# A merged weight conversion, fewer summing transfers and other times for side work, in a kernel of attention and two expert networks

## The chip, the core and the metric

The kernel runs on one core of a Trainium2 chip. A core has TensorE (matmuls, into PSUM), VectorE and ScalarE (elementwise work), GpSimd and a queue of transfers on SyncE. The metric is the device time of one execution, in microseconds (us). Times are compared as medians of repeated runs on the same chip.

## What is computed

Attention over 4 batches of 8 heads, 576 tokens and 64 columns each, in which every score below the row's maximum less tau is dropped, and behind it two networks on all 2304 tokens. The weights come as 64-bit floats.

```python
scores = scale * np.matmul(q, k.transpose(0, 1, 3, 2))
thresh = np.max(scores, axis=-1, keepdims=True) - tau
scores = np.where(scores >= thresh, scores, -1000000000.0)
...                                    # softmax, then
x = np.matmul(attn, v)                 # (2304, 512)
h = x @ w_in                           # (512, 2048)
x = (np.maximum(h, 0) + alpha * np.minimum(h, 0)) @ w_out
h = x @ w2_in
out = (h * (1 / (1 + np.exp(-h)))) @ w2_out
```

## The kernel before, in words

**Attention.** 16 pairs of heads, each with 9 tiles of 128 rows, so 144 steps. A step takes its scores on TensorE (L596), scales them and finds the maximum on VectorE (L610, 576 elements from PSUM), takes the exponential on ScalarE (L623) and masks and sums on VectorE (L636). Transposes (L670) and the products with v (L704, L711) follow. TensorE's order is the table ORDER; the function plan places the other engines' work by costs and priorities.

**Networks.** Tokens are in three blocks of 768 (p), the hidden layer in four groups of 512 (g), so each network (m) has 12 blocks of work, 24 in all. Both matrix products of a block are done by a scheme of seven products in place of eight: L482 runs 12 matmuls of 384 columns for each of the seven, on operands that are sums and differences of quarters. The first group of the first network alone has its second product done plainly (L966). Every 32-bit operand is split in two parts of reduced precision: a copy on ScalarE (L322) and the difference (the "split", L433 for weights, L472 for x, L1018 for the hidden layer), which may run on VectorE or GpSimd (both_step); three products of parts are summed.

**Weights.** Each group has eight chunks (four of w_in, four of w_out), 64 in all. The function conv turns a chunk's 64-bit floats into 32 bits: the magnitude's upper word through Abs with a scale on ScalarE (L404, into its own tile cm), the low word's top bits (L405), the sign put in (L407) and the joining of both (L409), then four sums of 128 columns (L428, one of them L422 in some chunks) and two splits of 384 and 512 columns (L433). A plain chunk has one split of 512 (L415). Seven chunks are converted during the attention, beside its own work; WI, WS, WN and WT say at which steps. XO says from which step on the first pieces of x may be made there (L463 the differences, L472 their splits); plan chooses the engine.

**Order in the networks.** TensorE's order is fixed by the loops. The function plan_late orders the rest by due times: a step is due when its TensorE user is, less what follows it, less OFF of its kind. It gives a both_step to GpSimd only with enough slack (POOL_SLACK), or, where PK allows, when much else waits for VectorE. Instructions marked port=True and GpSimd's work are kept apart by it, as users of one port. In the first network some sums of hidden tiles (acc, L1024) are not made by an engine but by a transfer that accumulates (L1029, issued from GpSimd); DSUM names which. Pieces of x are stored to DRAM in group 0 (L1117) and loaded again in the later groups (L1119), through four or five buffers xs.

## Time and profile before

| | us |
|---|---|
| median of 3 runs | 1019.19 (1013.49 to 1019.28) |
| profiled execution | 1022.07 |
| its span, first to last instruction | 1020.3 |
| TensorE busy in the span | 995.0 |
| VectorE busy | 899.1 |
| ScalarE busy | 658.9 |
| GpSimd busy | 214.5 |
| mean granted TensorE clock | 0.991 of full |

Matmuls are pipelined and their ends are modelled, so a busy TensorE is not one at its peak; counting matmuls in a stretch shows more. In the rows below PE is TensorE, PEld its weight loads, DVE VectorE, ACT ScalarE and POOL GpSimd; a row's `out<-in` names tiles, and L numbers are lines of the kernel. An arrow `<-` in a list of waits leads to the engine and line that ended the wait.

### The profile page before, as it was taken

Reading aid. Unit: us, or ns where it says so; the run is one execution under the profiler, and the core shown is the slowest. Engines: PE = TensorE matmul, PEld = TensorE weight load, DVE = VectorE, ACT = ScalarE, POOL = GpSimd, SP = SyncE. Lnnn points to the kernel's source line nnn. Section 1 sums busy time; section 2 is a strip of 40 time slices with the busy share of each in tenths; the row PEclk is TensorE's granted clock in tenths of the full one; section 3 lists DMA queues with packets and bytes.
Section 4 is the critical chain, followed back from the end, with each engine's and each line's share of the span. In section 5 each row is a group of like instructions: output and inputs, shape, how many; then the busy total and the mean of one; then the engine's idle time right before and its main releaser. Section 6 shows DMA issues by size and latency. Waiting matters only on the chain.

```text
span 1020.3 us, 16812 instructions
## 1 busy us (share of the span) xinstructions
PE 995.0 (98%) x6045; PEld 881.8 (86%) x6045; DVE 899.1 (88%) x1928; ACT 658.9 (65%) x1252; POOL 214.5 (21%) x163
## 2 busy tenths in 40 slices
PE   9999999999999998999999999889999999999998
PEld 5666665666579998999999999889999999999997
DVE  7999999999789876989799989799998999989666
ACT  6898888888776755555465546577676556555442
POOL 0000100000013102442533443522212231222011
PEclk9999999999999999999999999899999999999999
DMA  3222222221565776687777776455677776664743
GB/s 113 75 100 90 85 69 85 87 67 45 200 239 212 262 282 197 212 288 273 258 250 262 230 270 220 168 220 196 230 275 248 249 256 224 230 237 170 250 164 109
DMA packets 46916, 196.41 MB, mean 193 GB/s; under 512 B 5488, under 2 KB 8688, under 8 KB 46832
## 3 DMA queue, kind: packets, MB, share of 16 engines
q1 hardware_dynamic: 43936, 187.97, 51.7%
q0 software_dynamic: 2592, 7.08, 3.8%
q8 instruction: 48, 0.79, 0.3%
q10 hardware_dynamic: 304, 0.28, 0.1%
q14 instruction: 36, 0.29, 0.1%
HBM read 150.48 MB, written 37.75 MB: 184 GB/s over the span
## 4 chain that ended last, share of the span: by engine, by line
PE 84%; DVE 9%; DMA 3%; ACT 2%; issue 2%; ACTq 0%; DVEq 0%
PE ab L482 25%; PE c L482 16%; PE y L482 15%; PE s L596 8%; PE t L670 7%; PE pv L704 6%; PE y L966 5%; DMA xs<-xd 2%; DVE e L636 1%; DMA r<-r 1%; PE t L711 1%; DVE x L610 1%; PE t L676 1%; DVE xs L472 1%; DVE g L1018 1%
## 5 line engine op out<-in xcount | busy, mean ns | idle before, releaser
L482 PE MATMUL ab<-xs,w 128*128 128x384 f32 x1728 | 316.7, 337 | 7.7 <-DMA xs<-xd 3.9
L482 PEld LDWEIGHTS ab<-xs,w 128*128 128x128 f32 x1728 | 301.6, 189 | 12.6 <-issue 3.9
L482 PE MATMUL y<-g,w 128*128 128x384 f32 x840 | 159.6, 338 | 0.9 <-DVE X L983 0.9
L482 PEld LDWEIGHTS y<-g,w 128*128 128x128 f32 x840 | 149.5, 191 | 1.2 <-DVE X L983 1.2
L322 ACT ACTIVATE g<-r 128x768 fp32r<-128x768 f32 (+1 forms) x143 | 111.9, 795 | 50.3 <-PE c L482 15.9
L1018 POOL TENSOR_TENSOR g<-r,g 128x768 fp32r<-128x768 f32 x47 | 86.7, 1848 | 189.6 <-DVE ce L407 60.4
L482 PE MATMUL c<-g,w 128*128 128x384 f32 x612 | 117.0, 339 | 4.3 <-DVE g L1018 4.3
L610 DVE TENSOR_SCALAR_CACHE_REDUCE x<-s,nsc 128x576 f32<-128x576 f32 x144 | 112.6, 816 | 7.1 <-PE s L596 6.7
L322 ACT ACTIVATE su<-ab 128x384 f32<-128x384 f32 x144 | 70.1, 489 | 74.6 <-PE ab L482 69.8
L482 PEld LDWEIGHTS c<-g,w 128*128 128x128 f32 x612 | 108.1, 190 | 5.4 <-DVE g L1018 5.2
L983 DVE TENSOR_TENSOR X<-y,X 128x384 f32<-128x384 f32 x150 | 81.2, 552 | 27.8 <-PE y L482 27.6
L623 ACT ACTIVATE e<-x,m 128x576 f32<-128x576 f32 x128 | 96.7, 785 | 8.5 <-DVE x L610 8.3
L596 PE MATMUL s<-raw 64*128 64x288 f32 (+1 forms) x576 | 101.0, 429 | 0.6 <-DVE x L610 0.5
L636 DVE SCALAR_TENSOR_TENSOR e<-x,m,e 128x577 f32<-128x577 f32 x128 | 100.2, 813 | 1.1 <-ACT m L630 1.1
L596 PEld LDWEIGHTS s<-raw 64*128 64x128 f32 (+1 forms) x576 | 57.7, 188 | 38.9 <-DVE x L610 11.0
L482 PE MATMUL c<-xs,w 128*128 128x384 f32 x432 | 83.2, 341 | 3.5 <-ACT r L937 3.0
L322 ACT ACTIVATE pt<-t 128x512 f32<-128x512 f32 x128 | 70.5, 605 | 17.7 <-PE t L670 17.4
L482 PEld LDWEIGHTS c<-xs,w 128*128 128x128 f32 x432 | 77.1, 192 | 4.4 <-ACT r L937 3.3
L670 PEld LDWEIGHTS t<-ident,e 128*128 128x128 f32 x576 | 63.2, 141 | 20.2 <-issue 8.9
L670 PE MATMUL t<-ident,e 128*128 128x128 f32 x576 | 79.4, 278 | 0.2 <-DVE e L636 0.2
L1018 DVE TENSOR_TENSOR g<-r,g 128x768 fp32r<-128x768 f32 x74 | 71.3, 966 | 8.2 <-ACT g L322 7.9
L704 PE MATMUL pv<-pt,rv 128*64 128x512 f32 x256 | 62.4, 604 | 0.0
(110 smaller groups left out, 1447.6 us busy)
## 6 DMA issues: line engine op xcount, KB each, us to landing
xs<-xd SPq DMA_DIRECT2D x126, 768.0 KB, 6.1
xd<-xs SPq DMA_DIRECT2D x42, 768.0 KB, 3.6
raw<-in_w1i SPq DMA_DIRECT2D x16, 512.0 KB, 5.2
raw<-in_w1o SPq DMA_DIRECT2D x16, 512.0 KB, 4.7
raw<-in_w2i SPq DMA_DIRECT2D x16, 512.0 KB, 4.4
raw<-in_w2o SPq DMA_DIRECT2D x16, 512.0 KB, 4.3
rv<-in_v SPq DMA_DIRECT2D x16, 480.0 KB, 3.6
r<-r POOLq DMA_DIRECT2D x18, 384.0 KB, 7.5
```

Source lines behind the costliest of these rows:

```text
L322: e.activation(out=dst, in_=src, func=AF.Copy)
L472: st.append(both_step(2 * HN, src[1] + key, key, lambda e: e.tensor_tensor(out=xtile(slot)[:, 1], in0=src[0](), in1=xtile(slot)[:, 0].bitc ...
L482: T.matmul(bank, WT_[ws[c]][:, x, AI[a], :], xs[:, y, c, :], start=start and k == 0, stop=stop and k == 5, skip_group_check=True,)
L596: T.matmul(SP[u + k][:, hf, :S // 2], RAW[i][p, 0, q], RAW[i][p, 1, c], start=True, stop=True)
L610: V.tensor_scalar(out=x.rearrange("p (a b) -> p a b", a=2), in0=SP[u][:, :, :S // 2], scalar1=nsc, scalar2=None, op0=ALU.mult, op1=ALU.min ...
L623: A.activation(out=ES[u], in_=xts[u % XB][:, 1:S + 1], func=AF.Exp, bias=mcol(u, 0), scale=-1.0)
L636: V.scalar_tensor_tensor(out=e, in0=x, scalar=mcol(u, 1), in1=e, op0=ALU.is_le, op1=ALU.mult, accum_out=mcol(u, 2))
L670: T.transpose(TP[n][:, c * 128:(c + 1) * 128], EP[i, t // 2][:, o:o + 128], ident)
L704: T.matmul(AV[i][h * 64:(h + 1) * 64], RV[i][:, h, kt], src, start=kt == 0, stop=kt == KT - 1)
L966: T.matmul(yt, wview(ws[f])[:, a, i * 128:(i + 1) * 128], half(gs[f, k])[:, c], start=n == 0, stop=n == 3 * G - 1)
L983: V.tensor_tensor(out=dst, in0=src, in1=dst, op=ALU.add))))
L1018: add(*both_step(2 * HN, kr + kg, kg, lambda e: e.tensor_tensor(out=x[:, 1], in0=RP[n], in1=x[:, 0].bitcast(F32), op=ALU.subtract)))
```

## The change

The four parts of a chunk and its four sums now lie in one tile cw of eight columns of 128, of which cv and ce are the two halves. Abs writes into cv itself. L407, a two-source operation on 32-bit words, becomes a one-source operation on 16-bit halves (L408 of after), and L405 (L406) works on 16-bit halves too: one fills the lower half of each word, the other the upper. Two of the four sums, which subtract the same part, become one of 256 columns, except in the chunks with L422. One copy and one split of 896 columns, over seven neighbouring columns of cw, replace two each. So that these lie side by side, the host's order of the parts, the order of the seven weight operands (AI) and the signs of two differences of x are changed; weights are tracked by one key in place of two.

DSUM now goes by group: accumulating transfers make 12 of the sums where they made 18. The attention's seven chunks start at steps 34 to 94, ten apart, and the first pieces of x may start at step 114 instead of 84. The planner's due times and its rules for GpSimd have new numbers. TensorE's order is the same but for six matmuls of a first-network product that stand some 90 matmuls earlier in the attention's last steps.

```diff
@@ -33,13 +33,13 @@
-WI = 20
-WT = 4
+WI = 34
+WT = 12
...
-WS = 14
-WN = 6
-XO = 60
+WS = 10
+WN = 7
+XO = 30
...
-DSUM = (7, 4)
+DSUM = ((), (4,), (4,), (6, 4))
...
-OFF = {"w": 23.9, "x": 2.0, "t": 5.4, "y": -4.4}
-PK = 1e9
-PB = 0.6
+OFF = {"w": 21.5, "x": 1.8, "t": 2.2, "y": -2.4}
+PK = 0.3
+PB = 0.0
...
-POOL_SLACK = 5.03
+POOL_SLACK = 3.28
...
-AI = {"11": 0, "12": 1, "22": 2, "S1": 3, "S2": 4, "S3": 5, "S4": 6}
+AI = {"11": 0, "12": 1, "22": 2, "S1": 3, "S3": 4, "S2": 5, "S4": 6}
@@ -349,7 +349,8 @@
-    cm, cv, ce = (big.tile([128, 512], F32, name=n) for n in ("cm", "cv", "ce"))
+    cw = big.tile([128, 8, 128], F32, name="cw")
+    cv, ce = (cw[:, i:i + 4].rearrange("p a b -> p (a b)") for i in (0, 4))
...
@@ -395,43 +396,36 @@
         n = wslot(kind, gi, j)
         w, key = WT_[n], ("w", n)
         raw = raws[r]
-        low, top = raw[:, :, 0], raw[:, :, 1]
-        im, iv, ie = (x.bitcast(I32) for x in (cm, cv, ce))
+        top, half = raw[:, :, 1], raw.bitcast(U16)
+        iv, ie, he = cv.bitcast(I32), ce.bitcast(I32), ce.bitcast(U16).rearrange("p (f two) -> p f two", two=2)
         rk = ("raw", r)
         st = [
             dma_step(524288, [], [rk], lambda: nc.sync.dma_start(
                 raw, src.bitcast(I32).rearrange("p (f two) -> p f two", two=2))),
-            act_step(512, [rk], ["cm"], lambda: A.activation(out=cm, in_=top.bitcast(F32), func=AF.Abs, scale=2.0**-112)),
+            act_step(512, [rk], ["cv"], lambda: A.activation(out=cv, in_=top.bitcast(F32), func=AF.Abs, scale=2.0**-112)),
             dve_step(512, [rk], ["ce"], lambda: V.tensor_scalar(
-                out=ie, in0=low, scalar1=29, scalar2=None, op0=ALU.logical_shift_right), 0.35, port=True),
-            dve_step(512, [rk, "ce"], ["ce"], lambda: V.scalar_tensor_tensor(
-                out=ie, in0=top, scalar=-(2**31), in1=ie, op0=ALU.bitwise_and, op1=ALU.bitwise_or), port=True),
-            dve_step(512, ["cm", "ce"], ["cv"], lambda: V.scalar_tensor_tensor(
-                out=iv, in0=im, scalar=3, in1=ie, op0=ALU.logical_shift_left, op1=ALU.bitwise_or), port=True),
+                out=he[:, :, 0], in0=half[:, :, 1], scalar1=13, scalar2=None, op0=ALU.logical_shift_right), 0.35, port=True),
+            dve_step(512, [rk], ["ch"], lambda: V.tensor_scalar(
+                out=he[:, :, 1], in0=half[:, :, 3], scalar1=0x8000, scalar2=None, op0=ALU.bitwise_and), 0.35, port=True),
+            dve_step(512, ["cv", "ce", "ch"], ["cv"], lambda: V.scalar_tensor_tensor(
+                out=iv, in0=iv, scalar=3, in1=ie, op0=ALU.logical_shift_left, op1=ALU.bitwise_or), port=True),
         ]
-        if plain:
-            w, ks = wview(n), [(key, 0), (key, 3)]
-            st.append(act_step(512, ["cv"], ks, lambda: one(A, w[:, 0], cv)))
-            st.append(both_step(512, ["cv"] + ks, ks, lambda e: e.tensor_tensor(
-                out=w[:, 1], in0=cv, in1=w[:, 0].bitcast(F32), op=ALU.subtract)))
-            return st
-        v4 = cv.rearrange("p (a b) -> p a b", a=4)
-        s4 = ce.rearrange("p (a b) -> p a b", a=4)
-        a11, a12, a22, a21 = (v4[:, i] for i in range(4))
-        if flip:
-            st.append(port_step(128, ["cv", "ce"], ["ce"], lambda: V.scalar_tensor_tensor(
-                out=s4[:, 0], in0=a21, scalar=-1.0, in1=a22, op0=ALU.mult, op1=ALU.subtract)))
-            sums = ((2, a21, a11, ALU.subtract), (1, a22, s4[:, 2], ALU.add), (3, a12, s4[:, 1], ALU.subtract))
-        else:
-            sums = ((0, a21, a22, ALU.add), (1, s4[:, 0], a11, ALU.subtract), (2, a11, a21, ALU.subtract), (3, a12, s4[:, 1], ALU.subtract))
-        for i, x, y, op in sums:
-            st.append((both_step if both else port_step)(128, ["cv", "ce"], ["ce"], lambda e=V, i=i, x=x, y=y, op=op: e.tensor_tensor(
-                out=s4[:, i], in0=x, in1=y, op=op)))
-        for a, z, x, k in ((0, 3, v4[:, 0:3], "cv"), (3, 7, s4, "ce")):
-            n = 128 * (z - a)
-            st.append(act_step(n, [k], [(key, a)], lambda a=a, z=z, x=x: one(A, w[:, 0, a:z], x)))
-            st.append(both_step(n, [k, (key, a)], [(key, a)], lambda e, a=a, z=z, x=x: e.tensor_tensor(
-                out=w[:, 1, a:z], in0=x, in1=w[:, 0, a:z].bitcast(F32), op=ALU.subtract)))
+        x, z, k = cv, wview(n), ["cv"]
+        if not plain:
+            x, z, k = cw[:, 1:8].rearrange("p a b -> p (a b)"), w.rearrange("p a b c -> p a (b c)"), ["cv", "ce", "ch"]
+            a21, a11, a12, a22, s1, s3, s2, s4 = (cw[:, i] for i in range(8))
+            if flip:
+                st.append(port_step(128, ["cv", "ce", "ch"], ["ce"], lambda: V.scalar_tensor_tensor(
+                    out=s1, in0=a21, scalar=-1.0, in1=a22, op0=ALU.mult, op1=ALU.subtract)))
+                sums = ((s3, a21, a11, ALU.subtract), (s2, a22, s3, ALU.add), (s4, a12, s2, ALU.subtract))
+            else:
+                sums = ((s1, a21, a22, ALU.add), (cw[:, 5:7], cw[:, 0:5:4], a11.unsqueeze(1).to_broadcast([128, 2, 128]), ALU.subtract), (s4, a12, s2, ALU.subtract))
+            for o, a, b, op in sums:
+                st.append((both_step if both else port_step)(256 if len(o.shape) == 3 else 128, ["cv", "ce", "ch"], ["ce"], lambda e=V, o=o, a=a, b=b, op=op: e.tensor_tensor(
+                    out=o, in0=a, in1=b, op=op)))
+        st.append(act_step(512 if plain else 896, k, [(key, 0)], lambda: one(A, z[:, 0], x)))
+        st.append(both_step(512 if plain else 896, k + [(key, 0)], [(key, 0)], lambda e: e.tensor_tensor(
+            out=z[:, 1], in0=x, in1=z[:, 0].bitcast(F32), op=ALU.subtract)))
...
@@ -454,14 +448,13 @@
-            "T3": [(tA, b22, b12)], "T2": [(tA, tA, b11)], "T1": [(tB, b12, b11)], "T4": [(tA, b21, tA)],
+            "T3": [(tA, b12, b22)], "T2": [(tA, b11, tA)], "T1": [(tB, b12, b11)], "T4": [(tA, b21, tA)],
...
-            return [(("w", n), 0 if AI[a] < 3 else 3) for n in ws]
+            return [(("w", n), 0) for n in ws]
...
-                    if q in DSUM:
+                    if q in DSUM[self.g]:
...
-        w = [w[j, :, :, :, i] for i, j in ((0, 0), (0, 1), (1, 1), (1, 0))]
+        w = [w[j, :, :, :, i] for i, j in ((1, 0), (0, 0), (0, 1), (1, 1))]
```

What this does to the order, first on GpSimd in the attention (w are weight chunks, xs and r the pieces of x and their differences, X the attention's result, g hidden tiles of the networks). Before, from its first weight split on:

```order
L433 TENSOR_TENSOR w_76<-cv,w_76 128x384
L433 TENSOR_TENSOR w_77<-cv,w_77 128x384
L433 TENSOR_TENSOR w_77<-ce,w_77 128x512
L433 TENSOR_TENSOR w_78<-cv,w_78 128x384
L433 TENSOR_TENSOR w_79<-cv,w_79 128x384
L433 TENSOR_TENSOR w_79<-ce,w_79 128x512
L952 TENSOR_TENSOR g_3131<-r_3137,g_3131 128x384 x2
L472 TENSOR_TENSOR xs_3030<-r_3134,xs_3030 128x768
```

Now, from the same place on:

```order
L427 TENSOR_TENSOR w_76<-cw,w_76 128x896
L427 TENSOR_TENSOR w_77<-cw,w_77 128x896
L427 TENSOR_TENSOR w_78<-cw,w_78 128x896
L465 TENSOR_TENSOR xs_83<-X_73,xs_83 128x768
L456 TENSOR_TENSOR r_86<-X_73 128x768
L465 TENSOR_TENSOR xs_84<-r_86,xs_84 128x768
L456 TENSOR_TENSOR r_86<-X_73,r_86 128x768
L465 TENSOR_TENSOR xs_85<-r_86,xs_85 128x768 x2
```

Six splits of weights have become three of 896 columns, and the five operations of the first three pieces of x (L465 and L456, which are L472 and L463 of before) stand on GpSimd; before they stood on VectorE.

Second, VectorE at the start of the first network, around the two sums L1138 into TensorE's banks c (L405, L407, L409 and L415 convert one chunk). Before:

```order
L405 TENSOR_SCALAR ce<-raw_87 128x512
L1138 TENSOR_TENSOR c_3146<-c_3146,su_3139 128x384
L407 SCALAR_TENSOR_TENSOR ce<-raw_87,ce 128x512
L472 TENSOR_TENSOR xs_85<-r_86,xs_85 128x768
L409 SCALAR_TENSOR_TENSOR cv<-cm,ce 128x512
L1138 TENSOR_TENSOR c_3147<-c_3147,su_3141 128x384
L463 TENSOR_TENSOR r_86<-X_74 128x768
L415 TENSOR_TENSOR w_3124<-cv,w_3124 128x512
L472 TENSOR_TENSOR xs_3030<-X_74,xs_3030 128x768
```

Now (L406, L408, L410 and L427 convert; L1131 is L1138 of before, L465 is L472, L456 is L463, and L927, L1135 and L1141 are L934, L1142 and L1148):

```order
L406 TENSOR_SCALAR cw<-raw_87 128x512
L408 TENSOR_SCALAR cw<-raw_87 128x512
L1131 TENSOR_TENSOR c_3132<-c_3132,su_3125 128x384
L1131 TENSOR_TENSOR c_3133<-c_3133,su_3127 128x384
L927 SCALAR_TENSOR_TENSOR r_3121<-r_3121,neg,c_3132 128x384
L1135 TENSOR_TENSOR su_3125<-ab_2959,su_3125 128x384
L927 SCALAR_TENSOR_TENSOR r_3121<-r_3121,neg,c_3133 128x384
L1135 TENSOR_TENSOR su_3127<-ab_2960,su_3127 128x384
L927 SCALAR_TENSOR_TENSOR r_3123<-r_3123,neg,ab_2957 128x384
L927 SCALAR_TENSOR_TENSOR r_3123<-r_3123,neg,ab_2958 128x384
L1141 TENSOR_TENSOR ab_2959<-ab_2959,su_3126 128x384
L1141 TENSOR_TENSOR ab_2960<-ab_2960,su_3128 128x384
L410 SCALAR_TENSOR_TENSOR cw<-cw 128x512
```

The second sum stood behind the chunk's second and third operations and a split of x; now both sums follow the second operation, and the third comes eight instructions later.

Third, GpSimd where the first sums of hidden tiles begin (L1029 and L1022 are accumulating transfers, L1025 is L1032 of before, an addition; L428, L424 are sums of weight parts). Before:

```order
L433 TENSOR_TENSOR w_80<-ce,w_80 128x512
L433 TENSOR_TENSOR w_80<-cv,w_80 128x384
L1029 DMA r_3137<-r_3136 128x768
L1029 DMA r_3138<-r_3135 128x768
L428 TENSOR_TENSOR ce<-cv 128x128
L428 TENSOR_TENSOR ce<-ce,cv 128x128
L428 TENSOR_TENSOR ce<-cv 128x128
```

Now:

```order
L427 TENSOR_TENSOR w_76<-cw,w_76 128x896
L427 TENSOR_TENSOR w_78<-cw,w_78 128x896
L1025 TENSOR_TENSOR r_3121<-r_3121,r_3123 128x768
L1022 DMA r_3124<-r_3121 128x768
L1011 TENSOR_TENSOR g_3119<-r_3121,g_3119 128x768
L424 TENSOR_TENSOR cw<-cw 128x128
```

Of the first two transfers one has become an addition on GpSimd.

## Rows read from the trace of the kernel before

**Rows 1.** Page: busy us, share of the span, instructions of each engine.
```profile
PE 995.0 (98%) x6045; PEld 881.8 (86%) x6045; DVE 899.1 (88%) x1928; ACT 658.9 (65%) x1252; POOL 214.5 (21%) x163
```

**Rows 2.** Busy us (instructions) by stretch: PE, PEld, DVE, ACT, POOL, PEclk, DMA share, GB/s.
```profile
180.00:200.00 20.00, 20.00 (x148) 13.56 (x148) 19.85 (x56) 17.59 (x37) 1.29 (x1) 1.00 0.21 59
...
290.00:300.00 10.00, 8.42 (x46) 7.45 (x45) 10.00 (x17) 8.40 (x18) 1.43 (x2) 1.00 0.80 302
...
630.00:640.00 10.00, 10.00 (x59) 10.00 (x59) 10.00 (x20) 7.37 (x12) 3.67 (x3) 1.00 0.64 210
640.00:650.00 10.00, 7.01 (x29) 6.69 (x28) 9.42 (x17) 6.00 (x10) 3.15 (x3) 0.72 0.76 248
```

**Rows 3.** Timeline of VectorE and GpSimd in the attention: start, duration.
```profile
93.39 0.81 DVE L636 SCALAR_TENSOR_TENSOR e<-x,m,e 128x577 f32<-128x577 f32 x1
...
94.13 0.81 DVE L636 SCALAR_TENSOR_TENSOR e<-x,m,e 128x577 f32<-128x577 f32 x1
...
52.78 1.00 POOL L433 TENSOR_TENSOR w<-cv,w 128x384 fp32r<-128x384 f32 x1 [45.76 <-ACT w L322]
94.42 1.39 POOL L433 TENSOR_TENSOR w<-cv,w 128x384 fp32r<-128x384 f32 x1 [40.64 <-ACT w L322]
```

**Rows 4.** Conversion lines: duration in ns, minimum, median, maximum.
```profile
L405 DVE TENSOR_SCALAR ce<-raw x64: 411/421/1635, 46.5 to 933.5; 128x512 int32<-128x512 int32 x64
...
L407 DVE SCALAR_TENSOR_TENSOR ce<-raw,ce x64: 674/685/1921, 48.3 to 934.0; 128x512 int32<-128x512 int32 x64
```

**Rows 5.** Groups by line: busy us, mean ns of one, idle before.
```profile
L1018 POOL TENSOR_TENSOR g<-r,g 128x768 fp32r<-128x768 f32 x47 | 86.7, 1848 | 189.6 <-DVE ce L407 60.4 <-ACT g L322 22.1 <-DVE w L433 19.0
...
L428 DVE TENSOR_TENSOR ce<-cv 128x128 f32<-128x128 f32 x94 | 29.3, 311 | 0.2
...
L433 DVE TENSOR_TENSOR w<-cv,w 128x384 fp32r<-128x384 f32 x48 | 26.9, 561 | 1.3 <-ACT w L322 1.2
...
L472 DVE TENSOR_TENSOR xs<-X,xs 128x768 fp32r<-128x768 f32 x12 | 11.4, 951 | 3.7 <-ACT xs L322 3.7
...
L415 DVE TENSOR_TENSOR w<-cv,w 128x512 fp32r<-128x512 f32 x4 | 2.8, 689 | 0.0
```

**Rows 6.** Waits of TensorE: us in total, times, longest.
```profile
PE c L482 <- DVE g L1018: 4.3, 3, 2.0
PE ab L482 <- DMA xs<-xd: 3.9, 3, 2.8
PE c L482 <- ACT r L937: 3.0, 1, 3.0
```

**Rows 7.** Chain of waits, first network: start us, us, what.
```profile
395.57 9.51 DMA xs<-xd
...
405.21 3.88 PE ab L482 x12
```

**Rows 8.** Chain of waits, change of network.
```profile
643.45 1.28 ACT L937
...
645.28 4.21 PE c L482 x12
649.49 2.94 PE y L482 x12
...
717.96 2.68 PE c L482 x11
720.64 3.17 PE y L482 x12
723.81 2.08 PE ab L482 x12
```

**Rows 9.** Page: DMA issues, KB each, median us to landing.
```profile
r<-r POOLq DMA_DIRECT2D x18, 384.0 KB, 7.5
```

**Rows 10.** Timeline: one weight chunk's first operation and its last split.
```profile
396.77 0.42 DVE L405 TENSOR_SCALAR ce<-raw 128x512 int32<-128x512 int32 x1
...
410.28 1.29 POOL L433 TENSOR_TENSOR w<-ce,w 128x512 fp32r<-128x512 f32 x1 [6.39 <-ACT w L322]
```

More of the change, by code (lines that the diff above doesn't have):

```diff
@@ L456, in piece @@
         pre = {
-            "T3": [(tA, b22, b12)], "T2": [(tA, tA, b11)], "T1": [(tB, b12, b11)], "T4": [(tA, b21, tA)],
+            "T3": [(tA, b12, b22)], "T2": [(tA, b11, tA)], "T1": [(tB, b12, b11)], "T4": [(tA, b21, tA)],
         }.get(name, [])
-        sign = ALU.add if name == "T2" else ALU.subtract
         src = {"B11": b11, "B21": b21, "B22": b22, "T1": tB}.get(name, tA)
@@ L463, in piece @@
             st.append(both_step(2 * HN, x[1] + y[1], o[1], lambda e, o=o, x=x, y=y: e.tensor_tensor(
-                out=o[0](), in0=x[0](), in1=y[0](), op=sign)))
+                out=o[0](), in0=x[0](), in1=y[0](), op=ALU.subtract)))
         if not part & 2:
@@ L968, in mm @@
                             n += 1
-                reads = [(("w", x), h) for x in ws for h in (0, 3)] + [x for f in range(G) for x in gkeys(gs[f, k])]
+                reads = [(("w", x), 0) for x in ws] + [x for f in range(G) for x in gkeys(gs[f, k])]
                 add("PE", 12 * 0.1735, 12 * 0.1735 + 0.25, reads, [yk], mm)
@@ L1049, in pieces @@
                     lambda: split(2, r21, False),
-                    lambda: (sub(r11, r12, r11), sub(r12, r22, r12), split(7, r12, False)),
+                    lambda: (sub(r11, r12, r11), sub(r12, r12, r22), split(7, r12, False)),
                     lambda: (sub(r12, r22, r11), split(6, r12, False)),
@@ L1232, in rows @@
         w = plain.reshape(NG, 2, 2, 128, 2, 2, 128)
-        w = [w[:, :, i, :, j] for i, j in ((0, 0), (1, 0), (1, 1), (0, 1))]
+        w = [w[:, :, i, :, j] for i, j in ((0, 1), (0, 0), (1, 0), (1, 1))]
         w = np.stack(w).transpose(1, 4, 2, 3, 0, 5).reshape(NG, 2, 2, 128, 512)
```

## The prediction

> **What bounds the kernel now.** I read the page first: TensorE is busy for 995 of 1020 us, VectorE for 899 [rows 1]. One engine at 98% looks like the whole answer, but the second view, busy time by stretches, splits the program in two. In the attention VectorE has work for 19.85 of 20 us; in the two expert networks (MLP) TensorE runs without a gap for long stretches, and a few fall short [rows 2]. In the timeline of the attention two masks, VectorE's L636, start 0.74 us apart although each lasts 0.81: a VectorE instruction starts 0.08 before the one ahead ends, so it costs its duration less 0.08 [rows 3]. The attention's length is VectorE's work. By the timeline its last product ends at 281.8; after that only MLP products are left.
>
> In the MLP one step of 12 matmuls takes 2.08 us at full clock [rows 8]. All 4068 MLP matmuls (the counts of L482 and L966) at 2.08/12 are 705 us, some 4 of them inside the attention. The MLP part lasts 738, so some 37 us are lost there. The list of TensorE's waits and the chain of waits show where. A wait of over 1.7 us is followed by slow steps, which cost as much again; in the stretch with the longest, 640 to 650, the granted clock averages 0.72, so part of it ran at 1.2 instead of 2.4 GHz [rows 2, 8]:
> - start: 46 matmuls recorded from 290 to 300, 57.8 is full rate: 2.0 us, with VectorE at 10.0 of 10 [rows 2];
> - at 405: TensorE stands 2.8 us for a load of xs that took 9.5, and its next step takes 3.88 instead of 2.08: 4.6 us [rows 6, 7];
> - around the change from the first to the second network, 640 to 724. The first wait, on ScalarE, is 3.0, and its next two steps take 4.21 and 2.94 (3.0 too many): 6.0. Then come several waits on VectorE up to 2.0 [rows 6]; the one at 717 is followed by 11 matmuls in 2.68 and a step of 3.17, 1.9 too many [rows 8]. The five of them, added up from the timeline with their slow steps, are 9.8;
> - 4.0 after the last step, which the output's transfer takes, and the rest in small pieces.
>
> **The change part by part.** A weight chunk's second conversion operation (L407, two sources, 0.685) becomes a 16-bit operation with one source. Nothing in the trace is 16-bit. The lower bound is L405, the same kind of operation on 512 elements of 32 bits at a stride, 0.421; the upper one is L407 itself, 0.685, no gain [rows 4]. I take 0.42, the nearer shape: 0.26 us saved in each of 64 chunks. *VectorE: DVE Perf Modes* of the Trainium skill, in its section on what auto-detection checks, gives two results a cycle to a one-source operation in SBUF and more only to 16-bit data at step 1, which these are not; by it the new operation takes as long as L405, and the sum is the same.
>
> Where four sums become three, 0.31 each, the merged one has 256 elements and lies between the 128 and 384 elements of the rows, 0.43: less one overlap of 0.08, 0.1 saved per chunk [rows 5]. The two splits (384 elements 0.56, 512 elements 0.69) become one of 896, by the 1.0 ns per element between these 1.07: again 0.1 saved on VectorE [rows 5].
>
> *Attention.* Seven chunks are converted there, now from step 34 instead of 20. VectorE loses 7 times 0.26 (1.85), 4 times 0.1 (0.4), and one split of 896 takes the place of the two of 512 that stood on it (0.2). Its five operations on the first pieces of x (0.95 less 0.08 each: 4.35 [rows 5]) go to GpSimd, as the order there shows. Sum 6.8 us. With VectorE full, nothing else hides that work, so all of it could come off. But ScalarE is busy for 17.6 of 20 us [rows 2] and comes next, and a GpSimd operation of 1.85 [rows 5] is longer than two steps of 0.74 on VectorE beside it. I take **5 us** (bounds 0 and 6.8).
>
> *MLP start.* In VectorE's order the first block's second sum L1138 stood behind two conversion operations and a split of x (0.61, 0.61 and 0.87 [rows 4, 5]); now it follows the first sum directly, up to 2.1 us sooner. What is moved back for it is the rest of that chunk, due later. One of several stalls is touched. I take **1 us** (0 to 2.0).
>
> *Load at 405.* The load took 9.5 us [rows 7]. Its place in the queue and the number of buffers don't change. What shares the transfer engines does: in groups 1 and 2 one accumulating transfer (384 KB, 7.5 us [rows 9]) remains of two per block. The sums that they did come back as 6 operations on VectorE or GpSimd. I take **1.5 us** (0 to 4.6).
>
> *Change of network.* Of the first 6.0 us most is fixed: behind the product come the sum L1138 (0.56), the table load for the new activation (1.28 [rows 8]) and the activation (0.5), 2.3 of 3.0. TensorE's order there is the same, so it stays. The other 9.8 stand behind a VectorE that has no gap from 630 to 640 [rows 2]. Per group of three blocks (87.5 us) eight chunks save 8 times 0.26, 8 times 0.1 and 4 to 8 times 0.1, about 3.4; outside the attention 8 more operations of 768 elements leave VectorE (13 less in the order's counts, 5 of them above; the 6 sums in place of transfers are in that count), 0.8 per group. So VectorE has 4 us more room per group, and each of these waits of at most 2.0 begins shorter; one that vanishes takes its slow steps along. Since they follow each other within 65 us and GpSimd's longer operations hold some of it back, I take **4 us** (0 to 9.8).
>
> Where VectorE's relief falls into stretches in which TensorE has no gap, as from 500 to 600 and 800 to 1000, it is worth nothing: the 64 chunks' 0.46 and more are 30 us, and most of that is lost so.
>
> Sum: 5 + 1 + 1.5 + 4 = 11.5 us. The profiled execution took 1022.07 (span 1020.3 and 1.8 around it), so it would take 1010.6; it lay 2.9 above the median of the runs, 1019.19, and on the median the forecast is **1007.7**.
>
> **The rivals.**
> - *Backlog gone.* If 4 us per group are enough to clear all of the 9.8 and the attention gives its 6.8: 1019.2 - 6.8 - 1 - 1.5 - 9.8 = 1000. For it: the waits are short. Against: TensorE waits there on several engines in turn, so an earlier VectorE meets the next one.
> - *Only the attention gains.* The 16-bit operation runs at 0.685 after all (then the change doesn't do what it says, and the attention gives 3.6), or relief in the MLP meets new waits of the same size: 1019.2 - 5 = 1014. For it: most MLP stretches have no wait to take away.
> - *The shared port.* GpSimd gets 19 more operations of 768 elements, 1.85 each against 0.95 on VectorE [rows 5]. A L407 that met GpSimd took 1.92 instead of 0.685 [rows 4]. If each GpSimd operation held VectorE for its length, the attention's would hold 15.6 us (5 of 1.85, 3 of about 2.1) where the six of before add up to 7.2, which eats the 6.8; the MLP's 14 more (26 us) eat its relief of some 35: about 1019. Against: in the attention it was GpSimd that stretched, from 1.00 to 1.39, while the mask beside it kept 0.81 [rows 3]. *GPSIMD Engine Reference* of the skill (its specifications, and its table of what to run where) says that the two engines share SBUF interfaces when VectorE has two SBUF inputs, and that two-input work is about twice as slow there. The rows agree on both, but show the wait on either side, not always on VectorE.
> - *Slower: one work tile.* Before, a chunk's first operation (L404) wrote a tile of its own and ran ahead while the chunk before was summed and split. Now it writes where that chunk's split still reads, and the split waits for all sums. Behind other work a chunk took 14.8 us from L405 at 396.77 to the end of its last split at 411.57 [rows 10]. Eight chunks per 87.5 us allow 10.9 each; if they can no longer overlap, weights come late from there on. If each of seven group changes then had a wait like that at 717 (2.0 and 1.9 of slow steps), the time would be 1019.2 + 27 - 5 = 1041. Against: in the planner's table a chunk is due 21.5 us ahead of its use, and no TensorE wait of before is on a weight tile.
>
> **How the numbers follow.** Main case 0.48, backlog gone 0.16, attention alone 0.16, port 0.12, work tile 0.08. The main case by itself spans 1003 to 1012.5; three quarters of it lie below 1009, which is 1% under 1019.2 (about what a measurement can tell from no change). So faster: 0.36 + 0.16 = 0.52. Slower: the work tile and a bad end of the port, 0.10. The rest, 0.38, is within 1%. The range goes from 998, a little under the backlog case, to 1020, which takes in the port; left out are the work tile and the sum of all upper bounds.
>
> **What would show it.** L408 at 0.42 and a split of 896 at 1.07 confirm the prices; L408 near 0.69 makes the second rival. The attention's last product should end near 277 instead of 281.8; if it ends after 280 though GpSimd runs the five pieces, look for masks (L636 before) stretched over 0.82. At the change of network the wait behind the table load should still be there with about 3 us, the later ones on VectorE smaller or gone. The load of xs that held TensorE at 405 should hold it for less than 2.8. Waits of TensorE on w would make me wrong by the last rival.

## The result and the profile after

| | before | after |
|---|---|---|
| median, us | 1018.0 (4 runs, 1013.5 to 1019.3) | 1004.39 (4 runs, 1002.9 to 1005.4) |
| ratio after/before | | 0.9873, 95% interval 0.9838 to 0.9908 |
| profiled execution, us | 1022.07 | 1004.71 |
| VectorE busy, us | 899.1 | 875.5 |
| GpSimd busy, us | 214.5 | 244.9 |

Faster by 1.27%, 13.6 us. The forecast was 1007.7, 3.3 us too slow. The two traces differ by 17.4, because the profiled execution of before lay high: 29 runs of it beside the experiments have a median of 1018.44 and go from 1013.0 to 1023.3. Two runs far above all others (one of transfers_only at 2503 us, one of before at 5197) are left out of every median here.

The page of after, engines' busy time (answers [rows 1]):

```profile
PE 987.9 (98%) x6044; PEld 875.2 (87%) x6045; DVE 875.5 (87%) x1813; ACT 653.0 (65%) x1192; POOL 244.9 (24%) x170
```

Where the time went is read by comparing when the same products start. The table below takes the c<-xs products (L475, L482 before), counted off in order, from the timeline. Because the program's start moves the whole attention by up to 2.9 us from one trace to the next (that step starts at 17.99 in conv_only, at 20.90 in after_pieces_vector), each trace is counted from the start of its ninth attention step (L603, L610 before; 18.57 in before, 18.33 in after). An entry is how much later (+) or earlier (-) than in before that product starts; the column names are its times in before.

| profiled kernel | 287 | 400 | 434 | 552 | 610 | 640 | 678 | 712 | 744 | 978 |
|---|---|---|---|---|---|---|---|---|---|---|
| after | -2.6 | -3.2 | -6.8 | -7.5 | -6.9 | -7.4 | -10.2 | -14.4 | -17.5 | -17.5 |
| conv_only | +0.3 | 0.0 | -4.1 | +0.1 | +0.9 | +2.4 | -0.3 | -4.6 | -6.7 | -6.6 |
| numbers_only | +0.3 | -0.7 | -5.0 | -6.2 | -5.1 | -1.0 | -3.1 | +4.4 | +0.6 | +0.6 |
| after_old_planner | -2.6 | -3.2 | -7.2 | -6.1 | -0.2 | +2.2 | -1.1 | -5.6 | -7.4 | -7.3 |
| after_old_attention | +0.3 | -0.4 | -3.3 | -3.8 | -3.3 | -3.9 | -6.7 | -10.9 | -14.0 | -14.0 |
| after_pieces_vector | -0.9 | -1.7 | -6.2 | -6.7 | -6.0 | -6.6 | -10.8 | -14.9 | -18.1 | -18.1 |
| after_two_source | -0.6 | -0.3 | -3.5 | -4.4 | -3.2 | +3.6 | +0.7 | +11.2 | +7.3 | +7.3 |
| after_two_transfers | -2.6 | -3.5 | -7.3 | -6.9 | -2.9 | -3.6 | -7.3 | -11.4 | -12.8 | -12.8 |
| transfers_only | +1.6 | +1.2 | -2.3 | -2.0 | +1.0 | +3.0 | +0.1 | +1.4 | -2.1 | -2.0 |

So after gains 2.6 us in the attention, hardly anything at the start of the networks, 3.6 around 405, and 10.6 from 610 to 744, at the change of network. Behind 744 nothing moves.

Each row is one execution. The attention repeats well: six traces with after's attention stand between -2.6 and -2.7 at 287, two pairs that share another between +0.2 and +0.3. But transfers_only, in which VectorE runs the same instructions in the same order as in before there, stands at +1.6, and it ends 2.0 earlier than before although its median is later. So a difference of 2 us between two single traces need not come from the kernel.

TensorE's waits in after, whole span (total us, times, longest; answers [rows 6]):

```profile
PE ab L475 <- DVE r L927: 2.1, 1, 2.1
PE c L475 <- ACT r L930: 1.8, 1, 1.8
PE y L475 <- DVE X L976: 1.2, 1, 1.2
PE ab L475 <- ACT su L322: 0.9, 1, 0.9
PE ab L475 <- DMA xs<-xd: 0.8, 1, 0.8
PE c L475 <- DVE g L1011: 0.7, 2, 0.5
```

The first and fourth are at the start of the networks, new in place of five smaller ones. The fifth, on the load of xs, was 2.8 at 405. The waits on VectorE at 660 to 718 have shrunk to 0.4 at most; one of 1.2 at 650 is left.

TensorE in after at the change of network (timeline: start, us, instruction, in brackets the wait; answers [rows 8]), and busy time by stretches, first after's, then before's (the last columns are granted clock, transfer share and GB/s):

```profile
632.39 2.24 PE L475 MATMUL c<-xs,w 128*128 128x384 f32 x12
636.39 3.66 PE L475 MATMUL c<-xs,w 128*128 128x384 f32 x12 [1.76 <-ACT r L930]
639.85 2.56 PE L475 MATMUL y<-g,w 128*128 128x384 f32 x12
...
650.21 2.37 PE L475 MATMUL y<-g,w 128*128 128x384 f32 x12 [1.20 <-DVE X L976]
```

```profile
630.00:640.00 10.00, 8.24 (x39) 7.70 (x38) 8.80 (x17) 7.12 (x11) 4.09 (x3) 0.85 0.60 172
...
640.00:740.00 100.00, 98.17 (x558) 96.53 (x557) 96.38 (x155) 72.94 (x125) 27.20 (x16) 1.00 0.68 249
```

```profile
640.00:740.00 100.00, 90.94 (x481) 88.51 (x480) 90.08 (x152) 64.94 (x115) 30.25 (x17) 0.93 0.55 200
```

In the same 100 us TensorE does 77 matmuls more, at full clock, and VectorE is busier (96.4 against 90.1), not freer: the change shows here as work that arrives in time, not as a less busy VectorE.

### The profile page after: what moved, and what is told of

It reads as the page before. It is cut to its first block, busy times and chain, and to the rows that moved or that the text cites. A ratio compares the mean times of both kernels' runs of the same rounds, so it can differ in the third digit from the quotient of the medians.

```text
span 1002.9 us, 16663 instructions
## 1 busy us (share of the span) xinstructions
PE 987.9 (98%) x6044; PEld 875.2 (87%) x6045; DVE 875.5 (87%) x1813; ACT 653.0 (65%) x1192; POOL 244.9 (24%) x170
## 4 chain that ended last, share of the span: by engine, by line
PE 84%; DVE 8%; issue 3%; ACT 2%; DMA 1%; POOL 0%; ACTq 0%; DVEq 0%; POOLq 0%
PE ab L475 25%; PE c L475 16%; PE y L475 15%; PE s L589 8%; PE t L663 7%; PE pv L697 6%; PE y L959 5%; DVE e L629 1%; DVE x L603 1%; PE t L704 1%; DVE g L1011 1%; PE t L669 1%; DMA xd<-xs 1%; DMA xs<-xd 1%; DVE w L427 1%
## 5 line engine op out<-in xcount | busy, mean ns | idle before, releaser
L475 PE MATMUL ab<-xs,w 128*128 128x384 f32 x1728 | 314.3, 336 | 4.0 <-DVE r L927 2.1
L475 PEld LDWEIGHTS ab<-xs,w 128*128 128x128 f32 x1728 | 300.2, 188 | 7.2 <-ACT cw L405 2.4
L475 PE MATMUL y<-g,w 128*128 128x384 f32 x840 | 157.6, 335 | 1.2 <-DVE X L976 1.2
L475 PEld LDWEIGHTS y<-g,w 128*128 128x128 f32 x840 | 147.1, 188 | 1.7 <-DVE X L976 1.5
L1011 POOL TENSOR_TENSOR g<-r,g 128x768 fp32r<-128x768 f32 x57 | 105.2, 1851 | 174.2 <-ACT g L322 34.7
L603 DVE TENSOR_SCALAR_CACHE_REDUCE x<-s,nsc 128x576 f32<-128x576 f32 x144 | 112.4, 814 | 7.4 <-PE s L589 6.9
L475 PE MATMUL c<-g,w 128*128 128x384 f32 x612 | 115.6, 336 | 1.5 <-DVE g L1011 0.7
L475 PEld LDWEIGHTS c<-g,w 128*128 128x128 f32 x612 | 106.6, 188 | 3.6 <-DVE g L1011 1.3
L475 PE MATMUL c<-xs,w 128*128 128x384 f32 x432 | 82.3, 339 | 1.8 <-ACT r L930 1.8
L475 PEld LDWEIGHTS c<-xs,w 128*128 128x128 f32 x432 | 76.5, 190 | 2.5 <-ACT r L930 2.1
L427 DVE TENSOR_TENSOR w<-cw,w 128x896 fp32r<-128x896 f32 (+1 forms) x56 | 65.2, 1164 | 8.4 <-ACT w L322 8.3
L322 ACT ACTIVATE w<-cw 128x896 fp32r<-128x896 f32 (+1 forms) x64 | 59.5, 930 | 13.5 <-POOL cw L424 6.5
```

The lines of the kernel that those rows point to most:

```text
L322: e.activation(out=dst, in_=src, func=AF.Copy)
L427: st.append(both_step(512 if plain else 896, k + [(key, 0)], [(key, 0)], lambda e: e.tensor_tensor(out=z[:, 1], in0=x, in1=z[:, 0].bitcast ...
L475: T.matmul(bank, WT_[ws[c]][:, x, AI[a], :], xs[:, y, c, :], start=start and k == 0, stop=stop and k == 5, skip_group_check=True,)
L603: V.tensor_scalar(out=x.rearrange("p (a b) -> p a b", a=2), in0=SP[u][:, :, :S // 2], scalar1=nsc, scalar2=None, op0=ALU.mult, op1=ALU.min ...
L1011: add(*both_step(2 * HN, kr + kg, kg, lambda e: e.tensor_tensor(out=x[:, 1], in0=RP[n], in1=x[:, 0].bitcast(F32), op=ALU.subtract)))
```

## The experiments

Twelve kernels. conv is the new weight conversion with everything that belongs to it; the numbers are three sets: attention (WI, WT, WS, WN, XO), transfers (DSUM), planner (OFF, PK, PB, POOL_SLACK).

| kernel | median, us | ratio to before |
|---|---|---|
| conv_only | 1013.86 | 0.9951 (0.9933 to 0.9969) |
| numbers_only | 1023.38 | 1.0047 (1.0028 to 1.0067) |
| numbers_old_weight_due | 1024.00 | 1.0063 (1.0041 to 1.0086) |
| transfers_only | 1020.54 | 1.0029 (1.0006 to 1.0052) |
| after_old_planner | 1015.38 | 0.9982 (0.9963 to 1.0001) |
| after_old_rule | 1010.81 | 0.9919 (0.9887 to 0.9950) |
| after_old_due | 1010.99 | 0.9934 (0.9916 to 0.9952) |
| after_two_transfers | 1006.07 | 0.9882 (0.9848 to 0.9916) |
| after_no_transfers | 1012.96 | 0.9949 (0.9932 to 0.9966) |
| after_two_source | 1029.34 | 1.0106 (1.0067 to 1.0144) |
| after_old_attention | 1006.74 | 0.9883 (0.9851 to 0.9915) |
| after_pieces_vector | 1005.78 | 0.9875 (0.9839 to 0.9911) |

### The two halves of the change

conv_only is before with every hunk of the diff but those of the top numbers and of `DSUM[self.g]`; numbers_only is before with those alone.

> The kernel before with the new weight conversion alone (two 16-bit operations, the merged pair of sums, one split, one work tile, the signs that follow from it); the times of attention's side work, the sums by transfers and the planner's numbers stay as before. Theory 'relief': the 17.4 us come from work taken off VectorE by the conversion, so most of it shows here: 10 us at the change of network, 2 to 3 in the attention, 1004 to 1010 us. Rival 'order': the new numbers bring the gain by placing the work better, and the freed VectorE time falls where TensorE doesn't wait: 1012 to 1018 us. Rival 'one work tile': without chunks placed earlier in the plan the single tile makes weights late, and TensorE waits on w: over 1020 us.

> The kernel before with the new numbers alone (steps of attention's side work, one accumulating transfer fewer per block by group, the planner's due times and its rule for GpSimd), with the old conversion. Theory 'relief': the numbers only make use of VectorE time that the conversion frees; without it VectorE falls behind, and six sums per two groups come back on it: 1018 to 1030 us. Rival 'order': most of the gain shows here, 1006 to 1012 us. If the two add up, this run and the one with the conversion alone lose together 13 to 15 us.

Measured: the conversion alone gains 4.6 us, the numbers alone lose 4.9, together they gain 13.6. Both theories fall in their plain form: neither the relief nor the order has the gain to itself, and the two do not add up. What the numbers alone cost stands in two rows of TensorE's waits from 540 to 740 and one of busy time from 662 to 687 (columns as before):

```profile
PE y L482 <- ACT w L322: 9.1, 1, 9.1
PE c L482 <- ACT r L937: 3.6, 1, 3.6
```

```profile
662.00:687.00 25.00, 16.79 (x97) 16.48 (x95) 23.82 (x40) 15.82 (x28) 7.33 (x4) 0.89 0.49 184
```

One weight tile is 9.1 us late at 688, behind a VectorE that works 23.8 of the 25 us before. GpSimd is busy for 254.9 us in that run, 40 more than in before, and VectorE is no freer for it (904.0 us against 899.1, by their pages; six sums have come back from transfers as well). conv_only has no wait on weights, so the rival 'one work tile' is out; it loses at other places (a load of xs at 434, 2.65; pieces of xs, next fence) what is not lost with the numbers added:

```profile
PE ab L475 <- DVE xs L465: 3.1, 2, 2.0
PE c L475 <- ACT r L930: 2.6, 2, 2.4
```

### The planner's numbers

```diff
-OFF = {"w": 21.5, "x": 1.8, "t": 2.2, "y": -2.4}
-PK = 0.3
-PB = 0.0
+OFF = {"w": 23.9, "x": 2.0, "t": 5.4, "y": -4.4}
+PK = 1e9
+PB = 0.6
...
-POOL_SLACK = 3.28
+POOL_SLACK = 5.03
```

after_old_planner has all of it, after_old_due the line OFF alone, after_old_rule the other three.

> The changed kernel with the planner's old due times and its old rule for GpSimd (23.9, 2.0, 5.4, -4.4; work goes to GpSimd by lateness alone). Theory 'relief': the waits at the change of network shrank because VectorE has less to do, whatever the order: within 3 us of 1004.4. Rival 'order': the order at 630 to 730 us was what counted, and 6 to 10 us of waits behind VectorE and the activation come back: 1010 to 1015.

> The changed kernel with the planner's old rule for what goes to GpSimd (by lateness with 5.03 us of slack, and never for a busy VectorE), the new due times kept. With the old rule and the old due times together it took 1015.4. Theory 'rule': GpSimd takes work when VectorE has earlier due work in front, which is what keeps VectorE in time at the change of network: 1010 to 1016 us here. Rival 'due times': 1003 to 1007.

> The changed kernel with the planner's old due times (23.9, 2.0, 5.4 and -4.4 us for weights, pieces, their sums and results), the new rule for GpSimd kept. Theory 'due times': the sums' earlier due of 5.4 us and the weights' of 23.9 put them ahead of results that TensorE waits for: 1010 to 1016 us here, with waits at 550 to 590 and 640 to 680 us. Rival 'rule': 1003 to 1007. If both this run and the one with the old rule stay under 1008, the two only cost together.

Measured: +11.0, +6.4 and +6.6 us over after. Neither half is the whole of it; they roughly add. Each half leaves VectorE's busy time nearly as it is in after (877.2 us with the old rule, 875.9 with the old due times, 875.5 in after), so these losses come from the order and not from how much VectorE has to do. 'Relief' falls. All old numbers together take 32 us off GpSimd as well and put 12.2 on VectorE (887.7), so in that run order and room both differ. With all of them the loss lies from 552 to 640 (-6.1 to +2.2 in the table). TensorE's three largest waits from 540 to 740 are:

```profile
PE c L475 <- ACT r L930: 2.8, 1, 2.8
PE y L475 <- DVE X L976: 2.1, 2, 1.8
PE c L475 <- DVE X L975: 1.5, 1, 1.5
```

Of them 1.8 of the second (at 566) and the third (at 643) lie in that stretch, with one of 1.2 at 639; the first, at 648, stands behind it, where before has one of 3.0. From 640 to 744 the same kernel still gains 9.6 us on before, as conv_only does (9.1). So the planner's numbers bring theirs between 552 and 640, and most of the gain in the last hundred us comes with the conversion. Not all of it is shown to be the conversion's: transfers_only, without it, gains 5.1 there on the same trace of before.

> The kernel with the new numbers alone (1023.4 us), with the weights' due time put back from 21.5 to 23.9 us ahead of their use. Theory 'weights late': the 9.1 us wait on a weight tile at 688 us came from conversions being due too late for the old, longer conversion; it goes, and the time falls to 1011 to 1016. Rival 'no room': VectorE had no gap from 662 to 692, so the wait moves to sums or pieces instead and the time stays above 1018.

```diff
-OFF = {"w": 21.5, "x": 1.8, "t": 2.2, "y": -2.4}
+OFF = {"w": 23.9, "x": 1.8, "t": 2.2, "y": -2.4}
```

Measured 1024.0. The wait on the weight tile stays, 9.10 as before, at 689.2. So my reading of numbers_only, that conversions were due too late, falls; this due time doesn't help where VectorE has no gap.

### How much room VectorE has

after_two_source takes only the cheap second operation away:

```diff
-            dve_step(512, [rk], ["ch"], lambda: V.tensor_scalar(
-                out=he[:, :, 1], in0=half[:, :, 3], scalar1=0x8000, scalar2=None, op0=ALU.bitwise_and), 0.35, port=True),
+            dve_step(512, [rk, "ce"], ["ch"], lambda: V.scalar_tensor_tensor(
+                out=ie, in0=top, scalar=-(2**31), in1=ie, op0=ALU.bitwise_and, op1=ALU.bitwise_or), port=True),
```

(and L406 works on 32-bit words again, as L405 did).

> The changed kernel with the conversion's two 16-bit operations replaced by the old pair on 32 bits (one source, then two sources: 0.42 and 0.69 us instead of 0.46 and 0.455), the merged sums, the single split and all numbers kept. That puts 0.19 us per chunk, 12 us over 64 chunks, back on VectorE. Theory 'VectorE's room decides at the change of network': waits come back there as in the kernel with the new numbers alone, 1010 to 1020 us. Rival 'the merged operations and the order do it': 1004 to 1008.

Measured 1029.3: 25 us more for 12.8 us of VectorE time in these two operations (L406 and L408 by their groups 75.8 us, 63.0 in after), more than expected, and slower than before. VectorE's whole busy time rose by 19.0 (894.5 against 875.5). TensorE's waits in it:

```profile
PE y L475 <- ACT w L322: 11.1, 2, 7.8
PE ab L475 <- ACT w L322: 3.8, 1, 3.8
PE c L475 <- ACT r L930: 2.7, 1, 2.7
```

Weights are late three times at 636 to 695, and VectorE is busy 21.8 of the 23 us from 672 to 695. In the changed kernel no wait of 0.2 us or more in the networks is on a weight tile.

The transfers were meant to change VectorE's work in both directions: with two per block six sums leave the engines, with none in groups 1 and 2 six come to them (0.95 us each on VectorE when alone).

```diff
-DSUM = ((), (4,), (4,), (6, 4))
+DSUM = ((), (), (), (6, 4))
```

(after_no_transfers; after_two_transfers has `DSUM = (7, 4)` and `if q in DSUM:` again, transfers_only is before with the new DSUM.)

> The changed kernel with no accumulating transfers in groups 1 and 2 (none, none, none, two per block) instead of one per block: six more sums on VectorE or GpSimd, about 5 us of VectorE time, six transfers of 384 KB fewer. Theory 'transfers delay the load' by itself: the 0.8 us wait at 400 us goes, runs spread under 2, 1002 to 1004 us. Rival 'VectorE's room decides': putting 12 us back on VectorE cost 25, so 5 us here bring waits back behind VectorE or late weights at 570 to 700 us: 1006 to 1015.

> The changed kernel with two sums per block by accumulating transfers in every group, as before (the products 7 and 4), instead of none, one, one and two. Theory 'transfers delay the load': the load of xs at 400 us is slow beside the accumulating transfers, so its wait comes back, 0.8 to about 2.8 with slow steps behind it: 3 to 4 us more, 1007 to 1009. Rival 'transfers are free': the load's gain of 4 us came from its issue being earlier; the time stays within 1.5 us of 1004.4, or falls by up to 2 since the sums leave VectorE.

> The kernel before with one change: sums by accumulating transfers by group (none, one, one, two) instead of two in all. Theory 'transfers delay the load': the wait of 2 us and more on a load of xs is gone and the runs spread less, as the changed kernel's do; but the six sums come back on a VectorE that is full, so waits at the change of network grow: 1014 to 1024 us, spread under 4. Rival 'transfers are free': spread stays near 10 us and the time moves less than 2.

Measured: none in groups 1 and 2 costs 8.6 us, and weights are late again; two per block costs 1.7, not more than the interval can tell; in before, the new DSUM alone costs 2.4. For after_no_transfers the rival's number came and its waits too; from 540 to 740:

```profile
PE y L475 <- ACT w L322: 2.3, 1, 2.3
PE c L475 <- ACT r L930: 2.1, 1, 2.1
PE y L475 <- DVE g L1011: 1.7, 1, 1.7
```

Its reason did not. Of the six sums (L1025) the planner gave five to GpSimd (16 of them there instead of 11) and one to VectorE (14 instead of 13), and it moved other work to GpSimd too. From the page of after_no_transfers, engines' busy time:

```profile
PE 988.3 (98%) x6044; PEld 875.6 (87%) x6045; DVE 878.8 (87%) x1812; ACT 653.3 (65%) x1192; POOL 270.3 (27%) x171
```

GpSimd is busy 25.4 us more than in after. VectorE has one instruction fewer and is busy 3.3 us more: its instructions take longer, as the weight split L427 that took 1.98 us instead of 1.09 at 665.57, beside GpSimd's operation from 664.74 to 666.60. With two transfers per block VectorE is not relieved either (876.7). So neither run tests how much room VectorE has; what they change is GpSimd's share and the order. transfers_only does load VectorE: five of its six sums stand there (L1032, 16 instead of 11), its busy time is 909.4 us against 899.1, and a weight tile is 2.5 us late at 685. It loses 2.4 us for these 10.3.

That transfers delay the load is not shown. Where two per block stand, each of the three traces has one wait of over 2 us on a load of xs (before 2.8 at 405, conv_only 2.65 at 434, after_two_transfers 2.2 at 550); of the eleven with fewer none has one over 1.5. But the place moves: from 400 to 434 conv_only and after_two_transfers, with two, gain as much on before as after does (4.1, 3.8 and 3.6 in the table). The best run of after_two_transfers (1003.8) is as fast as after. And the other sign failed: the runs were to lie within 4 us in transfers_only and within 2 in after_no_transfers; they span 8.1 and 6.2, and conv_only's, with two transfers, 4.3. From the chain of after_two_transfers, and of after at the place of [rows 7]:

```profile
541.45 8.25 DMA xs<-xd
549.70 0.14 issue
549.84 3.89 PE ab L475 x12
```

```profile
392.43 7.23 DMA xs<-xd
399.66 0.14 issue
399.79 2.32 PE ab L475 x12
```

### The attention

after_old_attention restores `WI = 20`, `WT = 4`, `WS = 14`, `WN = 6`, `XO = 60`. after_pieces_vector sends the pieces' operations to VectorE whatever the planner would choose:

```diff
+        def onv(st):
+            return [("DVE", *s[1:5], lambda fn=s[5]: fn(V)) if s[0] == "BOTH" else s for s in st]
...
-        xdone = [chain(("xa", n), piece(0, PROD[n][1], k), src) for k, n in enumerate(PORD[:XA])]
+        xdone = [chain(("xa", n), onv(piece(0, PROD[n][1], k)), src) for k, n in enumerate(PORD[:XA])]
```

(and the same around the steps of the chains "xt").

> The changed kernel with the old steps for attention's side work (weights from step 20 at every 14th, pieces of x from 60 steps before the end) instead of the new ones. Theory 'relief': the attention's gain of 2.9 us comes from VectorE work that the conversion saves, so at most 1 us of it goes: first product of block 0 at 284 to 285.5 us, 1004 to 1006 us in all. Rival 'order': the conversion alone left block 0 at 286.9, so here too 2.5 us come back: 286.5 to 287, 1006 to 1008 us.

> The changed kernel with the operations on the first pieces of x in the attention forced onto VectorE, where they stood before, instead of GpSimd. By the prediction's term (five operations, each 0.87 of a full VectorE) block 0 would start 4.4 us later, 288.7, and the time be near 1008. Rival 'shared port': the operations on GpSimd stretch VectorE's as much as they relieve it (one of 0.69 took 2.31 beside one of GpSimd), so block 0 starts within 1 us of 284.3 and the time stays near 1004.4.

Measured, counted from the ninth step: with the old times block 0 starts 2.9 us later than in after, so the whole gain of the attention is gone, and conv_only says the same (+0.3). 'Order' holds. With the pieces on VectorE it starts 1.7 later (-0.9 against -2.6). Uncounted it was 288.6, the very number I had expected, but 2.6 of that was a later start of the program. The planner answered this edit with one of its own: it gave one split of 512 columns, which VectorE makes in after, to GpSimd:

```profile
228.51 1.27 POOL L427 TENSOR_TENSOR w<-cw,w 128x512 fp32r<-128x512 f32 x1 [63.25 <-ACT w L322]
```

That takes 0.6 us (0.69 less 0.08) off VectorE again, so the run puts 3.7 back and not 4.35, and 1.7 of it shows: more than half is lost, less than the rival says. On the whole time the old attention costs 2.4 us, and its four runs all lie above after's four; for the pieces' 1.4 the runs overlap, and by 744 that trace stands level with after's.

What the port takes is read from VectorE's groups in the attention, 7 to 283 us (busy us, mean ns of one). The masks that write e in after, in before, and in after_pieces_vector:

```profile
L629 DVE SCALAR_TENSOR_TENSOR e<-x,m,e 128x577 f32<-128x577 f32 x128 | 102.2, 827 | 1.4 <-ACT m L623 1.1 <-ACT e L616 0.3
```

```profile
L636 DVE SCALAR_TENSOR_TENSOR e<-x,m,e 128x577 f32<-128x577 f32 x128 | 100.2, 813 | 1.1 <-ACT m L630 1.1
```

```profile
L629 DVE SCALAR_TENSOR_TENSOR e<-x,m,e 128x577 f32<-128x577 f32 x128 | 100.9, 817 | 2.4 <-ACT m L623 1.5 <-ACT e L616 0.8
```

And one meeting in after, in the timeline:

```profile
239.77 1.05 DVE L629 SCALAR_TENSOR_TENSOR e<-x,m,e 128x577 f32<-128x577 f32 x1
240.29 2.23 POOL L456 TENSOR_TENSOR r<-X,r 128x768 f32<-128x768 f32 x1
...
240.75 2.31 DVE L427 TENSOR_TENSOR w<-cw,w 128x512 fp32r<-128x512 f32 x1
```

The masks take 2.0 us more than in before, and the one split 1.6 more than its usual 0.69: 3.6 us on a VectorE that sets the length. In after_pieces_vector it is 1.8 (masks 0.7, one sum of a piece 2.04 instead of 0.95). Of the 2.6 by which the five pieces fall short of 4.35 the difference explains 1.8 and the moved split 0.6; 0.2 is left.

## Why the prediction was right and wrong

**Prices.** The groups of conversion operations in after's attention:

```profile
L408 DVE TENSOR_SCALAR cw<-raw 128x512 uint16<-128x512 uint16 x7 | 3.2, 459 | 0.0
L406 DVE TENSOR_SCALAR cw<-raw 128x512 uint16<-128x512 uint16 x7 | 3.2, 454 | 0.0
...
L424 DVE TENSOR_TENSOR cw<-cw 128x256 f32<-128x256 f32 x4 | 1.7, 424 | 0.1
...
L427 DVE TENSOR_TENSOR w<-cw,w 128x896 fp32r<-128x896 f32 x1 | 1.1, 1083 | 0.0
```

The split (1.07 forecast) and the merged sum (0.43) were right. The 16-bit operations take 0.455, not 0.42, and since both are of that kind a chunk saves 0.19 on them instead of 0.26. The second rival, that they would run at 0.69, is out; the experiment that put 0.69 back shows what it would have meant, 1029 and not 1014.

**Attention: 2.6, forecast 5 of 6.8.** The sum adds up once the deduction for ScalarE and GpSimd, which was too small, is put right: I took off 1.8, the port alone took 3.6 and the dearer 16-bit operations 0.5, and 6.8 - 3.6 - 0.5 is 2.7. The sign that I named for it came: the attention's last product ends at 280.1 instead of near 277, with masks stretched. The forecast didn't see, though, that the conversion brings nothing there by itself: without the new times both conv_only and after_old_attention stand at +0.3. With the first chunk at step 34, VectorE idles in the stretch from 40 to 80 (37.6 of 40 us busy, 39.65 in before), which is part of why the saving isn't all seen; how each of the five numbers contributes stays open.

**MLP start: 0.1 up to 345, forecast 1.** The second sum came sooner as read from the order, but the next instruction that TensorE needs, L927, then keeps it waiting 2.1 us, once. A wait took the place of the ones removed.

**Load at 405: 3.6 in the trace, forecast 1.5.** The load was issued 3.1 us earlier, but so was everything around it (-3.2 in the table at 400); what made the wait 2.0 shorter is that it took 7.2 instead of 9.5, and the step behind it 2.3 instead of 3.9. That fewer transfers did this isn't shown: with before's number of them conv_only and after_two_transfers gain as much here, and their long wait stands elsewhere. How much of it the median run of before has isn't known, as only one execution of it was profiled; the 3.8 us by which the traces differ more than the medians are of this size.

**Change of network: 10.6, forecast 4 of 9.8.** This is the step that failed, twice. I held 6.0 around the first wait to be fixed, counting the sum, the table load and the activation behind the end of the product. ScalarE's and VectorE's timeline in after show otherwise:

```profile
633.84 0.57 DVE L1131 TENSOR_TENSOR c<-c,su 128x384 f32<-128x384 f32 x1
...
634.55 1.28 ACT L930 ACT_TABLE_LOAD   x1
...
634.78 0.56 DVE L1131 TENSOR_TENSOR c<-c,su 128x384 f32<-128x384 f32 x1
...
635.84 0.49 ACT L930 ACTIVATE r<-c 128x384 f32<-128x384 f32 x1
```

The product runs from 632.39 to 634.63, and its first sum starts at 633.84, before it ends; the table load follows at once. In before both sums stood at 642.82, 0.5 behind the product's end at 642.29, behind a conversion operation:

```profile
642.22 0.68 DVE L407 SCALAR_TENSOR_TENSOR ce<-raw,ce 128x512 int32<-128x512 int32 x1
642.82 1.02 DVE L1138 TENSOR_TENSOR c<-c,su 128x384 f32<-128x384 f32 x2
```

So the wait is 1.8 instead of 3.0. And of the 9.8 I took 4, since an earlier VectorE would meet the next limit. It met none: of the five waits only 1.2, 0.2 and 0.4 are left. The rival *backlog gone* described this stretch better than the main case; the total came out between the two only because the attention gave less. Not all of the 10.6 is sure to be the change's: transfers_only, whose median is later than before's, gains 3.1 from 610 to 744 on this one trace of before.

**What I had not seen: the two engines and the order.** I priced VectorE's relief as a straight line, so many us of room for so many us of waits. Putting 12.8 us of VectorE work back cost 25, and weights late by 2 to 9 us are what stands behind such losses where a row shows it. That is the fourth rival's effect with another cause: not the single tile cw, since numbers_only has the old three tiles and the same wait, but a VectorE without a gap. Yet VectorE's busy time alone does not set the time: with the old due times it is 875.9 against 875.5, and 6.6 us are lost; in after_no_transfers it rises by 3.3, through GpSimd's work, and 8.6 are lost; in transfers_only it rises by 10.3, and 2.4 are lost. Each edit makes the planner order everything anew, so how much of the 25 us is room and how much order stays open.

**The base.** The forecast set the sum against the profiled execution and took 2.9 off for the median; over 29 runs it is 3.6. A smaller gain in the median than in the traces follows from it, and this step was right in kind. That the median came within 3.3 us is partly luck: the four terms missed by -2.4, -0.9, +2.1 and +6.6, errors that cancel in part, and for the profiled execution the forecast was 1010.6 where 1004.7 came. Taking 2.9 off also took it that after's profiled execution would lie as far above its median as before's; it lies 0.3 above.

## What to carry to other kernels

Where an engine feeds a chain of deadlines and has no gap, a saving need not be worth its own length: ask at which stretch the engine is full and whether something with a long way to its user, like a weight tile, is next to be late there. Try a cheaper operation and the scheduler's numbers together and each alone; here the halves gave -5 and +5 and the whole -13.6. Where a planner chooses the engines, look where the work went before an experiment is read: the sums that were to load VectorE went to GpSimd, and VectorE's own instructions grew longer beside it. And before two traces are subtracted, line them up at a point behind the program's start, and see how far apart runs of one kernel lie.

## What the runs showed of the hardware

The shared port holds one-source operations too. Two rows of after's networks, where L406 took 1.42 instead of 0.45:

```profile
749.73 1.86 POOL L1011 TENSOR_TENSOR g<-r,g 128x768 fp32r<-128x768 f32 x1 [1.03 <-DVE w L427]
...
750.51 1.42 DVE L406 TENSOR_SCALAR cw<-raw 128x512 uint16<-128x512 uint16 x1
```

It ends 0.34 behind the end of GpSimd's operation, as if it had waited for nearly all of it; the split at 240.75 likewise ends 0.54 behind one. *SBUF — State Buffer* of the Trainium skill, in its section on the two separate sides, says that whichever starts first holds the shared pair for a whole instruction and the other is blocked; the rows agree for VectorE. The attention's L603, which reads its scores from PSUM, was not stretched: its 144 instructions in after take 778 to 822 ns.

The same wait does not always cost the same clock. In the attention before and transfers_only run the same instructions, and TensorE waits 1.98 us in both, at the same place. First before, then transfers_only:

```profile
173.81 0.44 PE L676 MATMUL t<-ident,rb 128*128 128x128 f32 x2 [1.98 <-ACT rb L651]
174.09 1.04 PE L670 MATMUL t<-ident,e 128*128 128x128 f32 x8
```

```profile
174.33 0.61 PE L676 MATMUL t<-ident,rb 128*128 128x128 f32 x2 [1.98 <-ACT rb L651]
174.74 1.91 PE L670 MATMUL t<-ident,e 128*128 128x128 f32 x8
```

The granted clock from 165 to 185 is 1.00 in the first and 0.91 in the second, so part of that stretch ran at 1.2 instead of 2.4 GHz; it is where transfers_only falls behind by the 1.6 us of the table. The networks show the same. The first step behind the wait of 1.76 in after took 3.66 us, with a granted clock of 0.83 from 632 to 642; in after_pieces_vector a wait of 1.78 at the same product is followed by a step of 2.44 at full clock:

```profile
639.85 2.44 PE L475 MATMUL c<-xs,w 128*128 128x384 f32 x12 [1.78 <-ACT r L933]
```

And after's longest wait, 2.15 at 297, is followed by a step of 2.32. So the prediction's sentence that a wait of over 1.7 us is followed by slow steps holds for some of these waits and not for others, and no row shown here gives the reason.
